# Splitting PSUM copies by bank, spreading routing pieces, and turning token blocks by DMA crossbar in a fused attention and expert kernel

## The chip, the cores and the metric

The kernel runs on one core of a Trainium2 chip. A core has TensorE (PE: matmuls, and transposes as a matmul against an identity), VectorE (DVE), ScalarE (ACT), GpSimd (POOL) and SyncE (SP, which issues DMAs here), each with its own queue of instructions in order, and 16 DMA engines that all of them share. Matmul results land in PSUM, which has eight banks of 512 fp32 columns; everything else lies in SBUF or in HBM. The metric is the device time of one launch in microseconds (us).

## The reference, cut to what matters

Two stages follow each other. The first is attention with random features: for 8 batches and 8 heads of 576 rows by 64, q and k are projected by `omega` (128 features), cosine and sine are taken, and the products with `v` are divided by a row sum. The second routes each of the 4608 rows (512 wide) to one of 8 experts by a cosine score, and applies that expert's two matrices and a gate.

```python
def phi(x):
    proj = np.einsum('bhsd,md->bhsm', x, omega)
    return np.concatenate([np.cos(proj), np.sin(proj)], axis=-1) / np.sqrt(m)
q_p, k_p = (phi(q), phi(k))
kv = np.einsum('bhsm,bhsd->bhmd', k_p, v)
z = np.sum(k_p, axis=2)
num = np.einsum('bhsm,bhmd->bhsd', q_p, kv)
den = np.einsum('bhsm,bhm->bhs', q_p, z)
...   # den is kept away from zero
# x: num / den, laid out as 4608 rows of 8 heads x 64
...
xn = x / (np.linalg.norm(x, axis=-1, keepdims=True) + 1e-06)
logits = xn @ en.T / tau
expert_idx = np.argmax(logits, axis=1)
...   # gate_w: the softmax of the chosen expert
for e in range(E):
    mask = expert_idx == e
    h = np.maximum(x[mask] @ w1[e], 0.0)
    out[mask] = gate_w[mask, None] * (h @ w2[e])
```

## The kernel before: what the change touches

**Attention** runs in 32 steps; a step handles a pair of heads of one batch. The loop is staggered: in step n the matmuls of step n stand beside the finish of n - 1 and the projections of n + 1. For each step, raw rows of q and k are transposed on PE into `qreg`, a PSUM region of nine blocks of 128 columns that begins at a bank's edge, so that columns 0 to 511 are one bank and 512 to 1151 reach over two more. Then they are copied to SBUF, k (with the first q block beside the ninth k block) by one engine and the rest of q by ACT:

```python
def turns(m):
    t = raw.pop(m)
    for j in range(NCH if m + 1 >= 0 else 4):          # NCH = 9
        nc.tensor.transpose(qreg[:, j*P : j*P + P], t[:, j*P : j*P + P], ident)
    ...
def copy_k(m):
    t = pa.tile([P, 5 * P], FP32, tag="kT", name="kT", bufs=1)
    if m + 1 >= 0:
        if m in ROUTED:                                # steps 18 to 30
            nc.scalar.activation(t, qreg[:, 0 : 5 * P], AF.Copy)
        else:
            nc.vector.tensor_copy(t, qreg[:, 0 : 5 * P])
    ...
def copy_q(m):
    t = pa.tile([P, 4 * P], FP32, tag="qT", name="qT", bufs=1)
    nc.scalar.activation(t, qreg[:, 5 * P :], AF.Copy)
```

`proj_k` and `proj_q` multiply these by `omega`; `whole_turns` (ACT) rounds the angle, `frac` (DVE) takes the rest, `fold` (DVE) its magnitude, `wave` (ACT) the sine, for both the sine and the cosine. The finished rows go to an HBM table `x_rows`, 512 fp16 values and a gate each.

**Routing** is small DVE work: `choose` and `choose2` pick the expert, `rank` and `places` give each token a slot, `block_hot` and `row_hot` build one-hot matrices with which PE inverts the placement, `block_experts` gives each block's expert, `root` (POOL) takes norms, `gates_a` to `gates_d` (DVE, with one tanh on ACT) compute the gates, `store_gates` (DMAs on SP) writes them into `x_rows`. It is done twice: for the first four batches, which fill blocks 0 to 10 (K1 = 11), within the attention steps 18 to 31 (`m` = n - 18 in `route_first`); and for all rows in the first expert blocks (`route_second`).

**Experts** follow as 40 blocks of 128 tokens of one expert each (and up to three more in a conditional part, not reached here). Rows are gathered from `x_rows` three to four blocks ahead, transposed on PE, and copied by ACT:

```python
def turn_x(j, eng):
    t = xin.pop(j)
    tr = bank(2 if j < 3 else 2 + 4 * (j % 2)).bitcast(FP16)
    for c in range(4):
        nc.tensor.transpose(tr[:, c*P : c*P + P], t[:, c*P : c*P + P].bitcast(FP16), ident16)
    move(eng, gpos[:, j : j + 1], t[:, D:XW].bitcast(FP32))     # the gate
    xT = late("kq", j % 2, 512)
    move(eng, xT, tr[:, 0:512])
    mo[j] = {"xT": xT}
...
def block(j, end):
    if j + 1 < end:
        hidden(j + 1, "act")        # 32 matmuls, relu by ACT into hT
    route_second_pe(j)
    if j < end - 2:
        turn_x(j + 2, "act")
    route_second(j)
    if j + 4 < NBLK:
        gather(j + 4)               # indirect DMA issued by POOL, three row buffers
    if j in (3, 4):
        for a in range(GRP1 * SG + SG * (j - 3), GRP1 * SG + SG * (j - 2), 3):
            root(a, a + 3)          # POOL
    result(j)                       # 8 matmuls, scaled by the gate on ACT
    if not LAST - 2 <= j < LAST:
        scatter(j)                  # indirect DMA issued by POOL
```

## Time and profile before

| | |
|---|---|
| time, median of 3 runs | 511.17 us (506.64 to 512.13) |
| the profiled execution | 485.76 us, span 483.9 us |
| PE busy | 462.3 us (96%) |
| PE weight loads busy | 387.8 us (80%) |
| POOL busy | 371.5 us (77%) |
| ACT busy | 357.8 us (74%) |
| DVE busy | 298.8 us (62%) |
| HBM traffic | 67.90 MB read, 15.22 MB written |

The span runs from the first to the last instruction of one profiled execution. Busy times of the engines overlap, and each is an average over stages that differ: which engine holds the others up has to be read stage by stage. Matmuls of PE are pipelined, so the duration of one overlaps the next; the time that a group takes is the distance between starts. In an answer that lists instructions, the columns are start, duration, engine, line of the kernel, operation, what it writes and reads, the count, and in square brackets the idle time before it and what ended that. In an answer of waits, a line has the waiting instruction, what it waited for, the total in us, the number of times, and the longest.

### The profile page before, as it was taken

What the parts mean: (1) busy time and instruction counts of PE and PEld (TensorE: products, weight loads), DVE (VectorE), ACT (ScalarE), POOL (GpSimd) and SP (SyncE); (2) the same over time, 40 slices, a digit from 0 to 9 for tenths busy, and PEclk for the clock granted to TensorE, in tenths of its full rate; (3) what the DMA queues carried; (4) which work ended last, traced back from release to release, by engine and by line L of the source; (5) the groups of instructions that cost most, each with busy time, mean ns of one, the idle gap of its engine ahead of it and who ended that gap; (6) DMA issues with size and microseconds to landing.
All of it is one profiled execution on the core that took longest, in us unless ns stands there. A gap on an engine that the chain in (4) does not pass through costs nothing.

```text
span 483.9 us, 18742 instructions
## 1 busy us (share of the span) xinstructions
PE 462.3 (96%) x7924; PEld 387.8 (80%) x7924; DVE 298.8 (62%) x506; ACT 357.8 (74%) x475; POOL 371.5 (77%) x472
## 2 busy tenths in 40 slices
PE   8899999999999999999999999889799999999993
PEld 7788889888888888888888888777577777777771
DVE  3688978889988888998888899969540000000000
ACT  3588788788788779989889979766366666666661
POOL 3599888998899998989999988866956555555552
PEclk9999999999999999999999999999989999999997
DMA  6279888787997878889779778423143223232211
GB/s 178 65 172 195 176 180 167 171 176 156 176 177 164 167 152 200 164 163 180 159 147 185 166 153 148 75 52 112 42 100 132 94 95 104 87 99 103 92 71 35
DMA packets 57652, 65.63 MB, mean 136 GB/s; under 512 B 29397, under 2 KB 37589, under 8 KB 57568
## 3 DMA queue, kind: packets, MB, share of 16 engines
q0 software_dynamic: 18064, 30.96, 33.7%
q1 hardware_dynamic: 39104, 32.95, 26.5%
q8 instruction: 65, 1.06, 0.9%
q10 hardware_dynamic: 400, 0.49, 0.4%
q14 instruction: 19, 0.16, 0.1%
HBM read 67.90 MB, written 15.22 MB: 172 GB/s over the span
## 4 chain that ended last, share of the span: by engine, by line
PE 54%; POOL 18%; DVE 12%; DMA 7%; ACT 5%; issue 3%; POOLq 0%; SPq 0%; ACTq 0%
PE ps L893 13%; PE ps L914 12%; PE ps L388 8%; PE ps L334 6%; POOL zt L321 5%; PE ps L260 4%; PE ps L224 3%; POOL zt L322 3%; POOL zs L324 3%; POOL zs L323 3%; DMA out_dram<-sik,prm 3%; PE ps L272 3%; DVE sik L297 2%; DMA kq<-in_q_dram 2%; DVE siq L297 2%
## 5 line engine op out<-in xcount | busy, mean ns | idle before, releaser
L893 PEld LDWEIGHTS <-w_sb 128*128 x1280 | 75.8, 99 | 10.3 <-issue 1.5
L893 PE MATMUL ps<-kq,w_sb 128*128 128x128 f16 x1280 | 79.0, 220 | 0.7 <-ACT kq L842 0.7
L388 PE MATMUL ps<-kv,siq 128*64 128x73 f32 x1152 | 76.4, 229 | 1.4 <-DVE kv L373 0.6
L914 PE MATMUL ps<-w_sb,cok 128*128 x320 | 76.2, 382 | 0.0
L388 PE MATMUL ps<-kv,coq 128*64 128x73 f32 x1152 | 74.9, 226 | 0.0
L388 PEld LDWEIGHTS ps<-kv,siq 128*64 128x64 f32 x1152 | 60.5, 135 | 5.3 <-ACT xb L422 0.7
L388 PEld LDWEIGHTS ps<-kv,coq 128*64 128x64 f32 x1152 | 61.1, 137 | 0.0
L811 POOL DMA_INDIRECT xin_all<-rf_x,prm x43 | 45.5, 1057 | 17.0 <-PE ps L850 9.6
L321 POOL TENSOR_TENSOR zt<-sik 128x512 f32<-128x512 f32 x32 | 41.2, 1287 | 22.3 <-ACT sik L310 21.9
L914 PEld LDWEIGHTS <-cok 128*128 128x128 f16 x320 | 29.8, 98 | 28.8 <-issue 0.4
L322 POOL TENSOR_TENSOR zt<-zt 128x256 f32<-128x256 f32 x64 | 48.9, 765 | 5.0
L297 DVE SCALAR_TENSOR_TENSOR sik<-sik,ps 128x1152 f32<-128x1152 f32 x32 | 43.2, 1349 | 7.1 <-ACT sik L293 6.9
L260 PE MATMUL ps<-omT,kT 64*128 64x128 f32 x576 | 45.1, 288 | 0.0
L297 DVE SCALAR_TENSOR_TENSOR siq<-siq,ps 128x1152 f32<-128x1152 f32 x32 | 43.1, 1347 | 1.8 <-ACT siq L293 1.7
L321 POOL TENSOR_TENSOR zt<-cok 128x512 f32<-128x512 f32 x32 | 42.8, 1339 | 0.0
L293 ACT ACTIVATE sik<-ps 128x1152 f32<-128x1152 f32 x32 | 36.2, 1132 | 8.1 <-PE ps L260 6.6
L310 ACT ACTIVATE siq<-siq 128x1152 f32<-128x1152 f32 x32 | 37.1, 1160 | 4.3 <-DVE coq L303 4.3
L293 ACT ACTIVATE siq<-ps 128x1152 f32<-128x1152 f32 x32 | 35.9, 1123 | 5.8 <-PE ps L280 5.8
L247 ACT ACTIVATE qT<-ps 128x512 f32<-128x512 f32 x32 | 19.1, 595 | 28.3 <-DVE kT L238 27.9
L260 PEld LDWEIGHTS ps<-omT,kT 64*128 64x128 f32 x576 | 39.1, 192 | 1.1 <-issue 0.5
L310 ACT ACTIVATE coq<-coq,consts 128x1152 f32<-128x1152 f32 x32 | 39.9, 1247 | 0.0
L310 ACT ACTIVATE cok<-cok,consts 128x1152 f32<-128x1152 f32 x32 | 39.9, 1247 | 0.0
(194 smaller groups left out, 1152.3 us busy)
## 6 DMA issues: line engine op xcount, KB each, us to landing
w_sb<-in_moe_w_dram POOLq DMA_DIRECT2D x32, 512.0 KB, 8.2
kq<-in_q_dram SPq DMA_DIRECT2D x62, 144.0 KB, 4.4
kq<-in_k_dram SPq DMA_DIRECT2D x62, 144.0 KB, 4.4
v<-in_v_dram SPq DMA_DIRECT2D x34, 144.0 KB, 3.9
rf_x<-xb SPq DMA_DIRECT2D x32, 144.0 KB, 7.3
xin_all<-in_v_dram SPq DMA_DIRECT2D x30, 144.0 KB, 4.8
xin_all<-rf_x,prm POOLq DMA_INDIRECT x43, 2.9
out_dram<-sik,prm POOLq DMA_INDIRECT x20, 3.0
```

What stands on the lines that cost most here:

```text
L247: nc.scalar.activation(t, qreg[:, 5 * P :], AF.Copy)
L260: nc.tensor.matmul(kreg[:, s * P : s * P + P], lhsT=t[r0 : r0 + 64, j * P : j * P + P], rhs=omT[r0 : r0 + 64], start=True, stop=True,)
L293: nc.scalar.activation(si, REG[nm], AF.Copy, bias=CMAGIC, scale=1.0)
L297: nc.vector.scalar_tensor_tensor(out=si, in0=si, scalar=CMAGIC, in1=REG[nm], op0=ALU.subtract, op1=ALU.subtract)
L310: nc.scalar.activation(t, t, AF.Sin, bias=pio2 if which == "co" else 0.0, scale=-TWO_PI * SINSC)
L321: nc.gpsimd.tensor_tensor(zt, t[:, 0:4], t[:, 4:8], ALU.add)
L322: nc.gpsimd.tensor_tensor(zt[:, 0:2], zt[:, 0:2], zt[:, 2:4], ALU.add)
L334: nc.tensor.matmul(kreg[64 * half : 64 * half + 64, 512 * hh : 512 * hh + P], lhsT=d["v"][r0 : r0 + 64, c], rhs=ph[r0 : r0 + 64, s * P : s ...
L388: nc.tensor.matmul(nm2[r0 : r0 + 64, a, (c - c0) * W : (c - c0) * W + W], lhsT=ph[:, s * P + r0 : s * P + r0 + 64], rhs=d["kv"][:, half, h ...
L811: ins = nc.gpsimd.indirect_dma_start(out=t, out_offset=None, in_=x_rows[:], in_offset=bass.IndirectOffsetOnAxis(ap=prm[:, j : j + 1], axis=0),
L893: nc.tensor.matmul(h_ps[:, f * P : f * P + P], lhsT=weights(k), rhs=d["xT"][:, c * P : c * P + P], start=(c == 0), stop=(c == 3),)
L914: nc.tensor.matmul(y_ps, lhsT=d["hT"][:, c * P : c * P + P], rhs=weights(NW1 + NW2 * (j % 2) + c), start=(c == 0), stop=(c == NW2 - 1),)
```

## The change

It has four parts. The first lets the two copies read different banks side by side, the second and third spread small routing work over steps and blocks, the fourth takes the transposes of the token rows from PE and their copies from ACT.

1. *Copies.* The k copy takes columns 0 to 511 of `qreg` (one bank), the q copy columns 512 to 1151 (two others); the ninth k block and the first q block now travel with q. In the prologue the same split holds, ACT takes part in the first copy, and DVE's copy comes ahead of its `frac`, while `fold` moves into step 0.
2. *First routing.* `block_experts` moves one step earlier, `gates_c` is halved over two steps, `choose` of group 2 moves one step later.
3. *Second routing.* The sums of squares of the last group move from block 2 to block 1, the roots on POOL from blocks 3 and 4 to blocks 0 and 2, and each `row_hot` is cut into three pieces.
4. *Transposes.* Rows of blocks 3 to 39 are transposed by a DMA through the crossbar, SBUF to SBUF, issued by SP in block j for block j + 3, straight into one of four buffers. For these blocks `turn_x` copies only the gate. PE transposes and their PSUM copies stay for blocks 0 to 2.

```diff
@@ -230,36 +230,34 @@
                 )
 
         def copy_k(m):
-            t = pa.tile([P, 5 * P], FP32, tag="kT", name="kT", bufs=1)
+            t = pa.tile([P, 4 * P], FP32, tag="kT", name="kT", bufs=1)
+            if m in ROUTED:
+                nc.scalar.activation(t, qreg[:, 0 : 4 * P], AF.Copy)
+            else:
+                nc.vector.tensor_copy(t, qreg[:, 0 : 4 * P])
+            st.setdefault(m + 2, {})["kT"] = t
+
+        def copy_q(m):
+            t = pa.tile([P, 5 * P], FP32, tag="qT", name="qT", bufs=1)
             if m + 1 >= 0:
-                if m in ROUTED:
-                    nc.scalar.activation(t, qreg[:, 0 : 5 * P], AF.Copy)
-                else:
-                    nc.vector.tensor_copy(t, qreg[:, 0 : 5 * P])
-                st.setdefault(m + 1, {})["t"] = t
+                nc.scalar.activation(t, qreg[:, 4 * P :], AF.Copy)
+                st[m + 1]["qT"] = t
             else:
-                nc.vector.tensor_copy(t[:, 0 : 4 * P], qreg[:, 0 : 4 * P])
-                nc.vector.tensor_copy(t[0:64, 4 * P :], qreg[0:64, 4 * P : 5 * P])
-            st.setdefault(m + 2, {})["kT"] = t
-
-        def copy_q(m):
-            t = pa.tile([P, 4 * P], FP32, tag="qT", name="qT", bufs=1)
-            nc.scalar.activation(t, qreg[:, 5 * P :], AF.Copy)
-            st[m + 1]["qT"] = t
-
+                nc.scalar.activation(t[0:64, 0:P], qreg[0:64, 4 * P : 5 * P], AF.Copy)
+            st[m + 2]["kT8"] = t
 
         KS = [c // 2 + 4 * (c % 2) if c < 8 else 8 for c in range(NCH)]
         QS = [8 if c == 0 else (c - 1) // 2 + 4 * ((c - 1) % 2) for c in range(NCH)]
 
         def proj_k(n):
-            t = st[n]["kT"]
             for j in range(5):
+                t = st[n]["kT"][:, j * P : j * P + P] if j < 4 else st[n]["kT8"][:, 0:P]
                 for par in range(2 if j < 4 else 1):
                     r0 = 64 * par
                     s = j + 4 * par if j < 4 else 8
                     nc.tensor.matmul(
                         kreg[:, s * P : s * P + P],
-                        lhsT=t[r0 : r0 + 64, j * P : j * P + P],
+                        lhsT=t[r0 : r0 + 64],
                         rhs=omT[r0 : r0 + 64],
                         start=True,
                         stop=True,
@@ -272,7 +270,7 @@
                 nc.tensor.matmul(
                     qreg[:, 512 * par : 512 * par + 512],
                     lhsT=omT[r0 : r0 + 64],
-                    rhs=d["qT"][r0 : r0 + 64],
+                    rhs=d["qT"][r0 : r0 + 64, P:],
                     start=True,
                     stop=True,
                 )
@@ -280,7 +278,7 @@
             nc.tensor.matmul(
                 qreg[:, 1024:1152],
                 lhsT=omT[64:P],
-                rhs=d["t"][64:P, 4 * P :],
+                rhs=d["qT"][64:P, 0:P],
                 start=True,
                 stop=True,
             )
@@ -528,6 +526,7 @@
         nc.vector.tensor_scalar(omT, tp_om, INV2PI, None, ALU.mult)
         turns(-2)
         copy_k(-2)
+        copy_q(-2)
         keep_warm(2)
         proj_k(0)
         nc.vector.tensor_scalar(emb_n[:E, 0:1], emb_n[:E, 0:1], 1e-6, None, ALU.add)
@@ -539,10 +538,9 @@
             )
         whole_turns(0, "k")
         turns(-1)
+        copy_k(-1)
         copy_q(-1)
         frac(0, "k")
-        fold(0, "k")
-        copy_k(-1)
         tp_e = ps[:, 6 * 512 : 6 * 512 + H * E]
         for h in range(H):
             nc.tensor.transpose(
@@ -843,15 +841,25 @@
             else:
                 nc.vector.tensor_copy(dst, src)
 
+        def turn_x_dma(j):
+            xT = late("kq", j % 4, 512)
+            nc.sync.dma_start_transpose(
+                out=xT.rearrange("p (c t) -> p c t", c=4), in_=xin[j][:, 0:D].bitcast(FP16)
+            )
+            mo[j] = {"xT": xT}
+
         def turn_x(j, eng):
             t = xin.pop(j)
+            if j in mo:
+                move(eng, gpos[:, j : j + 1], t[:, D:XW].bitcast(FP32))
+                return
             tr = bank(2 if j < 3 else 2 + 4 * (j % 2)).bitcast(FP16)
             for c in range(4):
                 nc.tensor.transpose(
                     tr[:, c * P : c * P + P], t[:, c * P : c * P + P].bitcast(FP16), ident16
                 )
             move(eng, gpos[:, j : j + 1], t[:, D:XW].bitcast(FP32))
-            xT = late("kq", j % 2, 512)
+            xT = late("kq", j % 4, 512)
             move(eng, xT, tr[:, 0:512])
             mo[j] = {"xT": xT}
 
@@ -1010,17 +1018,18 @@
                 gates_b(0, GRP1)
             elif m == 9:
                 row_hot(oh1, r1["lo"], 6, 12)
+                block_experts(0, K1, False, r1["a"])
             elif m == 10:
                 row_hot(oh1, r1["lo"], 12, S1)
-                block_experts(0, K1, False, r1["a"])
+                gates_c(0, 1)
             elif m == 11:
                 rows_of(r1["inv"], 0, K1, r1["a"])
-                gates_c(0, GRP1)
+                gates_c(1, GRP1)
             elif m == 12:
                 gates_d(0, GRP1)
                 store_gates(0, GRP1)
+            elif m == 13:
                 choose(GRP1)
-            elif m == 13:
                 square_rows(GRP1)
                 choose2(GRP1)
 
@@ -1050,10 +1059,12 @@
                 nc.tensor.addr_align(128, STEP_AT)
             if n < NS:
                 proj_q(n, place_first if n == NS - 1 else lambda: None)
+                fold(n, "k")
+                if n == 0:
+                    wave(n, "si", "k")
+                whole_turns(n, "q")
                 if n > 0:
-                    fold(n, "k")
-                whole_turns(n, "q")
-                wave(n, "si", "k")
+                    wave(n, "si", "k")
                 zsum(n, 0)
             if n == 0:
                 set_up_turn()
@@ -1160,6 +1171,7 @@
             elif j == 1:
                 squares(NS - 1, nc.vector)
                 square_sums(NS - 1)
+                square_rows(NGRP - 1)
                 r2["rk"] = r2["a"].take((NSLOT + 1) * E).rearrange("p (e s) -> p e s", e=E)
                 nc.vector.tensor_copy(r2["rk"], r2["ps"])
                 starts2(r2["rk"], NSLOT, r2["a"])
@@ -1167,13 +1179,14 @@
             elif j == 2:
                 r2["dest"] = places2(*r2["wg"], NSLOT, r2["a"])
                 r2["blk"], r2["lo"] = places3(r2["dest"], NSLOT, r2["a"])
-                square_rows(NGRP - 1)
             elif j == 3:
                 r2["rr"] = block_hot(r2["blk"], NSLOT, K1, NBLK - K1, r2["a"])
             elif j == 4:
-                row_hot(r2["oh"][0], r2["lo"][:, 0:18], 0, 18)
+                for a in range(0, 18, 6):
+                    row_hot(r2["oh"][0], r2["lo"][:, 0:18], a, a + 6)
             elif j == 5:
-                row_hot(r2["oh"][1], r2["lo"][:, 18:36], 0, 18)
+                for a in range(0, 18, 6):
+                    row_hot(r2["oh"][1], r2["lo"][:, 18:36], a, a + 6)
                 for part in (gates_a, gates_b, gates_c, gates_d):
                     part(GRP1, NGRP)
                 store_gates(GRP1, NGRP)
@@ -1188,10 +1201,12 @@
             if j < end - 2:
                 turn_x(j + 2, "act")
             route_second(j)
+            if 2 < j + 3 < LAST:
+                turn_x_dma(j + 3)
             if j + 4 < NBLK:
                 gather(j + 4)
-            if j in (3, 4):
-                for a in range(GRP1 * SG + SG * (j - 3), GRP1 * SG + SG * (j - 2), 3):
+            if j in (0, 2):
+                for a in range((GRP1 + j // 2) * SG, (GRP1 + j // 2 + 1) * SG, 3):
                     root(a, a + 3)
             result(j)
             if not LAST - 2 <= j < LAST:
```

More of the change, by code (lines that the diff above doesn't have):

```diff
@@ L232, in copy_k @@
         def copy_k(m):
-            t = pa.tile([P, 5 * P], FP32, tag="kT", name="kT", bufs=1)
-            if m + 1 >= 0:
-                if m in ROUTED:
-                    nc.scalar.activation(t, qreg[:, 0 : 5 * P], AF.Copy)
-                else:
-                    nc.vector.tensor_copy(t, qreg[:, 0 : 5 * P])
-                st.setdefault(m + 1, {})["t"] = t
-            else:
-                nc.vector.tensor_copy(t[:, 0 : 4 * P], qreg[:, 0 : 4 * P])
-                nc.vector.tensor_copy(t[0:64, 4 * P :], qreg[0:64, 4 * P : 5 * P])
+            t = pa.tile([P, 4 * P], FP32, tag="kT", name="kT", bufs=1)
+            if m in ROUTED:
+                nc.scalar.activation(t, qreg[:, 0 : 4 * P], AF.Copy)
+            else:
+                nc.vector.tensor_copy(t, qreg[:, 0 : 4 * P])
             st.setdefault(m + 2, {})["kT"] = t
         def copy_q(m):
-            t = pa.tile([P, 4 * P], FP32, tag="qT", name="qT", bufs=1)
-            nc.scalar.activation(t, qreg[:, 5 * P :], AF.Copy)
-            st[m + 1]["qT"] = t
+            t = pa.tile([P, 5 * P], FP32, tag="qT", name="qT", bufs=1)
+            if m + 1 >= 0:
+                nc.scalar.activation(t, qreg[:, 4 * P :], AF.Copy)
[3 more added lines that the diff above has]
+            st[m + 2]["kT8"] = t
         KS = [c // 2 + 4 * (c % 2) if c < 8 else 8 for c in range(NCH)]
```

## The prediction

> **What bounds the kernel now.** I read the page first: the slices of the span show one engine full nearly throughout.
>
> ```profile
> PE   8899999999999999999999999889799999999993
> ...
> DVE  3688978889988888998888899969540000000000
> ...
> DMA  6279888787997878889779778423143223232211
> ```
>
> TensorE (PE) is at nine tenths except at the start, at slices 25, 26 and 28, counted from 0 (within 302 to 351 us) and at the end. Slices 0 to 25 are the attention, the rest the expert blocks; in the latter the DMA engines are a third busy. The answer by windows gives the same for the steady expert blocks; its columns are busy time and count per engine, the clock, the DMA share and GB/s.
>
> ```profile
> 360.00:400.00 40.00, 40.00 (x468) 29.61 (x466) 0.00 (x0) 26.43 (x54) 23.50 (x23) 1.00 0.31 102
> 400.00:440.00 40.00, 40.00 (x471) 29.77 (x469) 0.00 (x0) 26.42 (x55) 22.44 (x22) 1.00 0.30 99
> ```
>
> PE is busy all 40 us of 40, ScalarE (ACT) 26, GpSimd (POOL) 23. What a block consists of is read from the timeline, starts in the first column:
>
> ```profile
> 440.25 1.95 PE L893 MATMUL ps<-kq,w_sb 128*128 128x128 f16 x32
> ...
> 441.42 1.01 POOL L941 DMA_INDIRECT out_dram<-siq,prm  x1 [1.39 <-ACT siq L934]
> ...
> 442.04 0.39 PE L850 MATMUL ps<-ident,xin_all 128*128 128x128 f16 x4
> ...
> 442.26 1.89 PE L914 MATMUL ps<-w_sb,cok 128*128 x8
> ...
> 442.73 1.03 POOL L811 DMA_INDIRECT xin_all<-rf_x,prm  x1 [0.30 <-PE ps L850]
> ...
> 443.99 1.95 PE L893 MATMUL ps<-kq,w_sb 128*128 128x128 f16 x32
> ```
>
> From start to start: first product 442.04 - 440.25 = 1.79 us, the four transposes 442.26 - 442.04 = 0.22 us, second product 443.99 - 442.26 = 1.73 us. A block is 3.74 us, and all of it is PE issuing back to back. So here each PE instruction removed is time removed.
>
> The ramp of the expert stage is different. From the waits and the timelines of 316 to 362 us:
>
> ```profile
> DVE lsq L150 <- POOL lsq L762: 4.7, 1, 4.7
> ```
> ```profile
> 335.95 1.87 POOL L811 DMA_INDIRECT xin_all<-rf_x,prm  x1 [0.30 <-PE ps L850]
> 337.85 4.92 POOL L762 TENSOR_TENSOR lsq<-lsq,pmh 128x3 f32<-128x3 f32 x3
> 342.95 2.52 POOL L941 DMA_INDIRECT out_dram<-siq,prm  x1 [0.18 <-issue]
> 345.77 1.03 POOL L811 DMA_INDIRECT xin_all<-rf_x,prm  x1 [0.30 <-PE ps L893]
> ```
> ```profile
> 350.60 0.40 PE L850 MATMUL ps<-ident,xin_all 128*128 128x128 f16 x4 [2.94 <-DMA xin_all<-rf_x,prm]
> 350.93 2.62 PE L914 MATMUL ps<-w_sb,cok 128*128 x8
> 353.34 2.92 PE L893 MATMUL ps<-kq,w_sb 128*128 128x128 f16 x32
> ```
>
> The square roots (L762) sit on POOL between two gathers, so block 8's gather starts only at 345.77; PE waits 2.94 us for it and then runs some matmuls at a lower clock. First product 7 starts at 344.66; with 1.79 + 36 inversions (1.1) + 0.22 + 1.73 the next would start at 349.5, but it starts at 353.34 and lasts about 1 us too long: **4.8 us lost**. The same roots hold VectorE (DVE) 4.7 us, and with it the gates; their store is issued from 352.83 by SyncE (SP).
>
> In attention the starts of the q projection (L272) follow each other by 9.22 us in most steps, with PE full. Summing what exceeds 9.22 over the steps gives 6.5 us: 0.5 in step 1, 2.3 in step 28, where DVE's routing delays PE, the rest in crumbs.
>
> **What the Trainium skill says.** "Advanced Engine Details and Errata", section "X-Bar Transpose (TRN2)": transposing DMAs run about as fast as plain ones, 350 to 400 GB/s; no transposing DMA is in this trace. "VectorE: DVE Perf Modes", section "The three transpose paths": 390 ns on TensorE against 1309 ns by crossbar for one 128x128; here a PE transpose shows 219 ns and costs 54 ns of issue. "SBUF — State Buffer", section "SBUF: two separate sides": while VectorE holds the shared port, GpSimd can't write DMA descriptors; the trace agrees: a gather or scatter takes 1.03 us alone, but 1.87 and 2.52 us beside DVE's long compares at 335 to 345 us. "TensorE: Matmul & The Clock Gate", section "Why this matters for your kernels": an idle gap over some 3 us lowers the clock; here 2.92 us instead of 1.95 after the gap.
>
> **The change, part by part.**
>
> 1. Transposes. 37 blocks (3 to 39) lose four PE transposes and one PSUM copy on ACT (0.6 us, off the path). On PE 37 x 0.215 = 8.0 us. Blocks 10 to 37 of the loop are steady: 28 x 0.215 = 6.0 us, which I count in full, at 3.52 us a block. The other nine (1.9 us) lie in the ramp, where a wait decides.
>
> Does the added DMA stay hidden? The gather of rows j+4 is issued about 2.3 us into block j (439.00 against 436.68) and lands 2.9 us later by the page: 1.7 us into block j+1. There SP issues the transpose; the first product needs it at the start of block j+3. At 3.52 us a block this leaves 2 x 3.52 - 1.7 = 5.3 us. A transpose moves 128 KB; at 350 GB/s that is 0.4 us, plus a fixed part which I take from the gathers' 2.9 us: 3 to 3.5 us, an estimate. It fits, and the DMA engines have two thirds free.
>
> 2. Ramp. The roots move to blocks 0 and 2, and row_hot is cut from 2304 to 768 columns an instruction, so POOL gets in between. That removes DVE's wait of 4.7 us: DVE ends its compares at about 344.8, and the gates (0.8 before the tanh, 0.4 on ACT, 2.1 after) end at about 348.3 instead of 352.8. But SP works in order, and in block 5 the four gate stores stand ahead of the transpose of block 8. They are issued from 348.4 and take 2.6 us (352.83 row: 2.58), so that transpose leaves at 351 and lands at 354. First product 8 then starts at about 354 where it started at 353.3. **A wait takes the place of the one removed**: with the 1.9 us of the nine PE transposes included, I book the ramp as 0.5 us worse.
>
> 3. Copies. The split at column 512 makes k read one PSUM bank and q two others. Before:
>
> ```profile
> ACT qT L247 <- DVE kT L238: 27.9, 18, 2.1
> ```
>
> ACT gets that back, and 0.1 us of longer copy per step against it. But those are steps at PE's 9.22 us, so nearly nothing of the 27.9 us is on the path. I book 0.7 us. At the start the q projection no longer waits for DVE's fold and copy: it can follow the warming matmuls at 13.2 instead of 13.84, and ACT does the first sine while it waits; 1.0 us.
>
> 4. First routing. Moving block_experts (2.0 us on DVE with its long last write) from step 28 to 27 takes it away from the inversion on PE, but lays it on step 27, where DVE has 0.4 + 1.1 us free. 0.8 us won. Choose goes into step 31 with choose2: 0.3 us lost.
>
> Sum: 6.0 - 0.5 + 0.7 + 1.0 + 0.8 - 0.3 = 7.7 us of the span. The timed median is 511.17 against 485.76 in the profiled run, 5% more. If the extra is slower PE, the gain grows with it to 8.1 us. Since the parts look tuned together, my ramp is more likely too dark than too bright; I add 1 us: 511.2 - 9 = **502 us**.
>
> **Rivals.**
>
> A. The crossbar doesn't keep up. If a transpose of 128x512 costs four times the skill's 1.3 us and they queue, the block becomes 5.2 us, and 30 blocks add 30 x 1.5 = 45 us: 550 us. The skill's bandwidth and the 30% DMA share speak against it; nothing in this trace can exclude it. A milder form: latency of 6 us, past the 5.3 us of slack; PE then waits some tenths every block and the 6 us are gone: 509.
>
> B. The ramp is better than I think: if the gates end earlier or the store's issue is shorter, most of the 4.8 us and the 1.9 us comes home: 496 to 497.
>
> C. POOL becomes the bound of the ramp: roots in block 2 coincide with DVE's 1.36 us multiplies and push the gathers of blocks 7 and 8 back by 3 us, to which the transpose's 3 us add: 506. The 4.92 us for three roots speak for it.
>
> **Range and chances.** Main case 500 to 504 (half), B 496 to 499 (a fifth), C and the milder A 505 to 510 (a fifth), A in full (a tenth or less). Medians differ by a few us among runs of the same kernel (506.64 to 512.13). Eight in ten: 495 to 510. Two per cent is 10.2 us, so below 501: 0.42 faster, 0.50 the same, 0.08 slower.
>
> **What would show it.** In the changed profile: PE transposes (L850 before) 12 instead of 160; blocks 3.52 us apart with PE full in the windows after 370 us; a transpose from issue to landing of 3 to 3.5 us; in block 7 a PE wait for the transpose of block 8, issued after the gate stores; no DVE wait for the roots; ACT's wait of 27.9 us gone with the attention steps still at 9.22 us. Wrong would be: blocks at 3.7 us or more with PE waiting for SP's DMA; gathers slowed by the transposes; no wait in block 7; attention steps shorter than 9.2 us.

## The result, and the profile after

| | us, median | range |
|---|---|---|
| kernel before | 511.65 | 506.64 to 512.39 |
| changed kernel | 488.12 | 486.59 to 489.71 |

The ratio is 0.956, interval 0.949 to 0.963: 23.5 us won, where I had forecast 9. The time lies below my range of 495 to 510.

Each later set of runs was made on one chip with the kernel before beside it, and that kernel took 487 us in some sets (483.6 to 495.3) and 508 us in others (504 to 516), without overlap; I call them **quick sets** and **slow sets**, and the comparison above is like a slow set.

The page of the changed kernel, slices of the span (PE, DVE, DMA as before):

```profile
PE   8999999999999999999999999788889999989992
...
DVE  3789788799878788989888998859620000000000
...
DMA  6299798897887888887878777325566464545541
```

PE is no fuller than in the page of before, DMA went from a third to a half in the expert blocks. The transposes are there as intended: 12 PE transposes instead of 160, and 37 by the crossbar. The span, 487.0 us, is even longer than the 483.9 of the page of before. So **the two pages don't show the gain at all**: the page of before is that of an execution that took 485.76 us, while the timed ones took 511. A window of the changed kernel (busy time and count for PE, PEld, DVE, ACT and POOL, clock, DMA share, GB/s):

```profile
400.00:440.00 40.00, 37.90 (x426) 27.31 (x425) 0.00 (x0) 19.36 (x44) 22.26 (x22) 1.00 0.53 130
```

PE has gaps of 2.1 us in 40, where before it had none. What was missing was a profile of the kernel before in a slow set. Experiment e9 below gave one, with a span of 511.1 us. The same window of it:

```profile
400.00:440.00 40.00, 36.31 (x410) 25.86 (x408) 0.00 (x0) 22.21 (x47) 19.28 (x20) 1.00 0.26 85
```

PE idles 3.7 us of 40, at a full clock. The starts of the first expert product of block 0, of block 10 and of block 39 cut each span in four:

| profile | to block 0 | blocks 0 to 10 | blocks 10 to 39 | one block | after 39 |
|---|---|---|---|---|---|
| before, its first page (like a quick set) | 314.4 | 47.4 | 108.4 | 3.74 | 13.7 |
| before, slow set (e9) | 320.5 | 50.0 | 126.9 | 4.38 | 13.7 |
| changed, its first page (the runs above) | 313.7 | 51.0 | 107.2 | 3.69 | 15.2 |
| changed, slow set (e5) | 311.5 | 52.8 | 106.4 | 3.67 | 15.1 |
| changed, quick set (e13) | 315.1 | 47.8 | 102.7 | 3.54 | 13.7 |

Of 24.1 us between the second row and the third, 19.8 come from the 29 steady blocks. The rest is 6.8 in attention (4.3 of it in two steps of 12.41 and 10.88 us, which take 9.39 and 9.60 in the first page of before; e12, of the same set as e9, doesn't have them), less 1.0 in the ramp and 1.5 at the end.

**Where the steady blocks lose 0.6 us.** The first page of before, one block; lines as in the prediction:

```profile
427.09 0.39 PE L850 MATMUL ps<-ident,xin_all 128*128 128x128 f16 x4
...
427.35 0.60 ACT L903 ACTIVATE cok<-ps 128x512 f16<-128x512 f32 x1 [0.30 <-PE ps L893]
...
427.94 0.59 ACT L842 ACTIVATE kq<-ps 128x512 f16<-128x512 f16 x1
...
429.04 1.67 PE L893 MATMUL ps<-kq,w_sb 128*128 128x128 f16 x27
```

L903 is the relu of the second half of a first product. ACT works in order, so the copy of turned rows (L842) stands behind it. The copy ends at 427.94 + 0.59 = 428.53, and PE needs it at 429.04: a slack of **0.5 us**, which I had not looked for because PE waited for nothing. The same stretch in the slow set (e9):

```profile
425.94 0.39 PE L850 MATMUL ps<-ident,xin_all 128*128 128x128 f16 x4
...
427.09 0.60 ACT L903 ACTIVATE cok<-ps 128x512 f16<-128x512 f32 x1 [1.19 <-PE ps L850]
...
427.83 0.60 ACT L842 ACTIVATE kq<-ps 128x512 f16<-128x512 f16 x1
...
428.48 1.95 PE L893 MATMUL ps<-kq,w_sb 128*128 128x128 f16 x32 [0.42 <-ACT kq L842]
```

The relu starts 1.15 us after the first transpose instead of 0.26, so 0.9 us later, the copy ends at 428.43, and PE starts 0.05 us after it, having waited. Nothing is slower in itself: the relu 0.60, the copy 0.60, the product 1.95 as before. Over the whole run, the waits of e9:

```profile
ACT cok L903 <- PE ps L850: 32.9, 28, 1.7
...
PE ps L893 <- ACT kq L842: 18.5, 34, 1.6
```

The steady blocks differ by 126.9 - 108.4 = 18.5 us. That PE's waits for the copy sum to 18.5 us as well is chance: 12.7 us of them (28 waits) lie in the steady blocks, the rest before, and a wait is counted only from the modelled end of the last matmul ahead of it. In the first page of before the same PE wait is 0.7 us, once.

**The relu is not the whole of it, and not the last to hold the copy.** The copy also waits for PE's signal that the transposes are done, and the traces keep the times of these signals. I give medians over the steady blocks, measured from the end of the work that the profile gives:

| | first product done | transposes done | second product done | transposes' end to next first product |
|---|---|---|---|---|
| before, first page | 0.01 | 0.01 | 0.01 | 1.56 = 0.01 + 0.45 + copy 0.59 + 0.51 |
| before, slow set (e9) | 0.90 | 1.41 | 0.01 | 2.14 = 1.41 + 0.08 + copy 0.60 + 0.05 |

In the first page the copy waits 0.45 us behind the relu, and 0.51 us are left over at the end. In e9 the signal of the transposes is late too, and in 27 of 29 blocks the copy starts 0.08 us after it; the relu has ended 0.05 us ahead of that signal. So the relu and the signal hold the copy for almost the same time, and the signal comes last. The 0.58 us between 1.56 and 2.14 are what a block becomes longer (median 4.30 against 3.74). The ends of matmuls are modelled in a profile, so it can't be told whether the work was done late or only its signal came late; but the second product, which follows both in PE's order, signals on time.

And the changed kernel in its first page. L911 is now the second relu, and the copy is gone:

```profile
442.35 2.06 PE L901 MATMUL ps<-kq,w_sb 128*128 128x128 f16 x32
443.44 0.60 ACT L911 ACTIVATE cok<-ps 128x512 f16<-128x512 f32 x1 [2.43 <-PE ps L922]
...
444.25 1.89 PE L922 MATMUL ps<-w_sb,cok 128*128 x8
```

This relu belongs to the product that began at 438.84 and gave way to the second product at 440.62; it starts 2.8 us after that, so it is even later. But PE doesn't wait for it at 442.35: that product reads the rows from the crossbar's buffer. The relu's output is read only by the second product at 444.25. The change did not make the signals punctual; it took the rows off the way from PE over a late signal and a copy on ACT back to PE.

### The profile page after: what moved, and what is told of

Its sections match the earlier page's. It is cut to its first block, busy times and chain, and to the rows that moved or that the text cites. A ratio compares the mean times of both kernels' runs of the same rounds, so it can differ in the third digit from the quotient of the medians.

```text
span 487.0 us, 18456 instructions
## 1 busy us (share of the span) xinstructions
PE 458.4 (94%) x7776; PEld 380.9 (78%) x7776; DVE 294.9 (61%) x511; ACT 341.6 (70%) x439; POOL 369.6 (76%) x472
## 3 DMA queue, kind: packets, MB, share of 16 engines
q8 instruction: 64, 1.05, 0.9%
## 4 chain that ended last, share of the span: by engine, by line
PE 67%; POOL 16%; DVE 5%; DMA 4%; issue 3%; ACT 2%; SPq 0%; POOLq 0%; ACTq 0%; DVEq 0%
PE ps L901 14%; PE ps L922 13%; PE ps L386 10%; PE ps L332 9%; PE ps L258 6%; PE ps L224 5%; POOL zt L319 5%; PE ps L270 4%; POOL zt L320 3%; POOL zs L321 3%; DMA kq<-xin_all 3%; POOL zs L322 2%; PE ps L361 2%; PE ps L353 2%; POOL xb L422 1%
## 5 line engine op out<-in xcount | busy, mean ns | idle before, releaser
L901 PEld LDWEIGHTS <-w_sb 128*128 x1280 | 75.0, 98 | 19.9 <-issue 11.4
L901 PE MATMUL ps<-kq,w_sb 128*128 128x128 f16 x1280 | 79.9, 219 | 8.2 <-DMA kq<-xin_all 3.7
L386 PE MATMUL ps<-kv,siq 128*64 128x73 f32 x1152 | 77.8, 231 | 1.4 <-DVE kv L371 0.6
L386 PE MATMUL ps<-kv,coq 128*64 128x73 f32 x1152 | 76.2, 228 | 0.0
L386 PEld LDWEIGHTS ps<-kv,siq 128*64 128x64 f32 x1152 | 61.4, 137 | 5.2 <-ACT siq L291 0.7
L911 ACT ACTIVATE cok<-ps 128x512 f16<-128x512 f32 x40 | 24.0, 600 | 38.9 <-PE ps L901 21.3
L949 POOL DMA_INDIRECT out_dram<-siq,prm x20 | 20.6, 1028 | 39.0 <-ACT siq L942 37.8
L291 ACT ACTIVATE siq<-ps 128x1152 f32<-128x1152 f32 x32 | 36.2, 1131 | 15.1 <-PE ps L278 15.1
L319 POOL TENSOR_TENSOR zt<-cok 128x512 f32<-128x512 f32 x32 | 43.5, 1359 | 0.0
L909 ACT ACTIVATE cok<-ps 128x512 f16<-128x512 f32 x40 | 23.9, 596 | 21.3 <-PE ps L901 19.7
```

Of the source, the lines that this page charges most:

```text
L291: nc.scalar.activation(si, REG[nm], AF.Copy, bias=CMAGIC, scale=1.0)
L319: nc.gpsimd.tensor_tensor(zt, t[:, 0:4], t[:, 4:8], ALU.add)
L386: nc.tensor.matmul(nm2[r0 : r0 + 64, a, (c - c0) * W : (c - c0) * W + W], lhsT=ph[:, s * P + r0 : s * P + r0 + 64], rhs=d["kv"][:, half, h ...
L901: nc.tensor.matmul(h_ps[:, f * P : f * P + P], lhsT=weights(k), rhs=d["xT"][:, c * P : c * P + P], start=(c == 0), stop=(c == 3),)
```

## Experiments

**Theory** (called the theory of the queue in some expectations): the gain is ACT's copy leaving the queue behind the late relu. **Rivals**: the transposes' own signal being late, so that the copy is held wherever it stands; the 8 us of PE work; the spread of the small work (parts 1 to 3); PE's fetching of instructions or the loads of expert numbers as the cause of the lateness; a crossbar that costs or gives something of its own.

### Four parts in a quick set: e1 to e4

e1 is the kernel before once more. e2 is the changed kernel without part 4:

```diff
-            if 2 < j + 3 < LAST:
-                turn_x_dma(j + 3)
```

e3 is the kernel before with part 4 alone (`turn_x_dma`, the early return in `turn_x`, four buffers, the two lines above), e4 the kernel before with part 1 alone.

> The kernel before, unchanged. Its profile took 485.8 us, its timed executions 506 to 512, while the changed kernel takes 487 to 490 with and without a profile. Theory 1 (the lost time of the timed executions lies in the program before itself, in a stage that the first profile happened to run without loss): a new profile shows about 505 to 512 us, and the windows show where, most likely in the expert blocks, longer than 3.74 us with PE waiting for nothing shown. Theory 2 (the first profile is an accident of another kind, such as another chip): profile and times both near 486 or both near 511 here, with every stage stretched by the same share.

> The changed kernel with PE transposes and PSUM copies for all blocks: parts 1 to 3 alone. If the crossbar transposes bring the gain (theory A): 506 to 509 us, near the kernel before. If the copies and the routing pieces bring it (theory B): 488 us or less, since in the profiles the expert blocks of the changed kernel are not shorter than before (3.7 us on average from 357 to 474 us, with PE waits of 0.3 to 0.75 us in them that nothing shown ends). If the size of PE's program matters (theory C, instruction fetch): times that follow neither, with PE waits for nothing shown in the profile.

> The kernel before with part 4 alone: crossbar transposes for blocks 3 to 39. Theory A: about 490 us. Theory B: 511 us or more, since the ramp with late roots and the transposes behind the gate stores is longer by some us. Theory C: PE waits in the expert blocks like those of the changed kernel, 0.3 to 0.75 us in every second block.

> The kernel before with part 1 alone: copies split at the bank's edge and the new order of the prologue. My prediction gave it 1.7 us. Theory A: 509 to 510 us. Theory B: 495 us or less, if the wait of 27.9 us of ACT for DVE's copy was what stretched the timed executions.

| | us | before | ratio and interval | blocks 0 to 10 | one block |
|---|---|---|---|---|---|
| e1 | 487.44 | 486.96 | 0.9996 (0.9972 to 1.0020) | 45.6 | 3.80 |
| e2 parts 1 to 3 | 481.95 | 486.96 | 0.9886 (0.9820 to 0.9952) | 44.8 | 3.74 |
| e3 part 4 | 487.40 | 486.96 | 1.0016 (0.9987 to 1.0046) | 54.8 | 3.52 |
| e4 part 1 | 486.51 | 486.96 | 0.9973 (0.9944 to 1.0002) | 45.7 | 3.80 |

Here the kernel before takes 487 us, not 511, and no part brings more than 6 us. That was the first sign that the gain isn't in the parts but in what they meet. Part 4 makes the blocks exactly as short as forecast, 3.52 us, and loses it all in the ramp. The waits of e3 show why (L903 is the first product there):

```profile
PE ps L903 <- DMA kq<-xin_all: 12.8, 2, 10.6
```

With the roots still late, SP issues the gate stores at 353.42, the transpose of block 8 leaves behind them at 356.13, and PE waits 10.6 us for it.

### The same in a slow set: e5 to e8

e5 is the changed kernel once more. e6 has parts 1 to 3, PE transposes as before, and the 37 crossbar transposes beside them into a buffer that nobody reads. e7 moves the crossbar transpose ahead of the routing piece, so ahead of the gate stores in SP's queue. e8 is the changed kernel with PE's instructions shifted against its fetches from block 7 on.

```diff
 # e6: crossbar transposes go to slots 2 and 3, PE's copies to 0 and 1
-            xT = late("kq", j % 4, 512)          # in turn_x_dma
-            mo[j] = {"xT": xT}
+            xT = late("kq", 2 + j % 2, 512)
-            xT = late("kq", j % 4, 512)          # in turn_x
+            xT = late("kq", j % 2, 512)
 # e7
-            route_second(j)
             if 2 < j + 3 < LAST:
                 turn_x_dma(j + 3)
+            route_second(j)
 # e8, first lines of block(j)
+            if j == 7:
+                nc.tensor.addr_align(256, 160)
```

> The changed kernel, unchanged, beside the kernel before on the chip of this call. So far parts 1 to 3 alone gave 482 us, part 4 alone 487, the kernel before 487. Theory D (the 4.4% belong to how the kernel before ran where it took 511, not to the program): the two kernels stand at 484 to 489 us here, ratio 0.99 to 1.01. Theory A (the change as a whole is worth 4%): a ratio near 0.956.

> Parts 1 to 3 with PE transposes, and beside them the 37 crossbar transposes into a buffer that nobody reads. It measures what the transfers cost others. If they cost nothing (my prediction): 482 us, as without them. If they delay PE's own instructions or the gathers (theory E): 485 to 490 us, with PE waits for nothing shown, or for gathers, in the expert blocks, which were clean at 3.74 us a block without them.

> The changed kernel with the crossbar transpose issued ahead of the routing piece of its block, so that block 8's no longer stands behind the four gate stores in block 5. If the gate stores hold it (my step 2 of the ramp): PE's wait for the transpose in block 7 goes, 2 to 5 us faster than the changed kernel. If the wait in block 7 comes from elsewhere (rows gathered late, the inversion waiting for DVE): no difference of more than 1 us.

> The changed kernel with PE's program padded once, at the start of block 7, so that what PE meets [...] (about every two blocks in the profile of the changed kernel, always within the first product) falls into the second product, where PE issues an instruction per 216 ns and has time. Theory C (PE waits for its own instructions): the waits for nothing shown from 370 us on vanish and the time falls by up to 5 us. If the waits come from something else: they stay where they are.

| | us | before | ratio and interval | blocks 0 to 10 | one block |
|---|---|---|---|---|---|
| e5 changed | 488.54 | 508.0 | 0.9568 (0.9506 to 0.9629) | 52.8 | 3.67 |
| e6 unread crossbar | 510.29 | 508.0 | 1.0016 (0.9988 to 1.0044) | 49.3 | 4.58 |
| e7 transpose ahead of gates | 483.79 | 508.0 | 0.9541 (0.9484 to 0.9598) | 46.4 | 3.67 |
| e8 shifted | 495.93 | 508.0 | 0.9709 (0.9647 to 0.9770) | 61.4 | 3.67 |

e5 repeats the gain. e6 has everything of the change except that the rows are still turned on PE and copied by ACT, and nothing is left of the gain: PE waits 25.8 us for that copy. Both of its expectations, 482 and 485 to 490 us, missed: they were made from the quick set. So the gain hangs on who brings the rows, not on parts 1 to 3. Its blocks (4.58) are longer than those of the kernel before (4.38), so the unread transposes may cost something; parts 1 to 3 quite alone weren't run in a slow set, and could be some us better than e6.

e7 has the lowest median of this set. Its profile shows the wait that the prediction named for the gate stores. From e5, then from e7:

```profile
347.39 3.49 SPq L798 DMA_DIRECT2D rf_x<-gate  x4
...
354.52 3.57 PE L901 MATMUL ps<-kq,w_sb 128*128 128x128 f16 x32 [6.16 <-DMA kq<-xin_all]
```
```profile
343.19 1.21 SPq L846 DMA_TRANSPOSE kq<-xin_all  x1
...
353.75 3.47 PE L901 MATMUL ps<-kq,w_sb 128*128 128x128 f16 x32 [2.24 <-DMA kq<-xin_all]
```

In e7 the transpose of block 8 leaves before the stores, and block 8 starts at 347.83 instead of 354.52 without a wait. A smaller wait for the next block's transpose, 2.24 us, remains. The ramp is 6.4 us shorter in the profiles. The medians of e5 and e7 differ by 4.7 us, but their ratios only by 0.0027, or 1.4 us, with intervals that overlap: how much time this order is worth isn't settled.

e8 was to test whether PE's fetches make the signals late. Its blocks stay as they are, and one PE wait of 11.5 us before block 8, for nothing that the profile shows, makes it slower. It says nothing for that rival and doesn't exclude it, as one shift isn't all shifts.

### Is it the copy, or the crossbar? e9 to e12

e9 is the kernel before, for its profile. e10 has parts 1 to 3 and no crossbar transposes, with the gate and the turned rows copied by DVE from block 10 on; e11 is the kernel before with that one edit; e12 is the kernel before with the loads of the expert numbers left out from block 10 on, so that all later blocks use the expert of block 9 and the output is not the reference's.

```diff
 # e10 (in the changed kernel without turn_x_dma's call) and e11 (in the kernel before)
-                turn_x(j + 2, "act")
+                turn_x(j + 2, "act" if j < 8 else "dve")
 # e12
-                expert_of(j + 2)
+                if j < 8:
+                    expert_of(j + 2)
+                else:
+                    eoff[j + 2] = eoff[j + 1]
```

> The kernel before once more, for its profile. So far one chip ran it in 487 us (A) and another in 508 us (B), and the changed kernel in 488.5 us on B. In the profile of the crossbar-unused run on B the blocks take 4.5 us; PE's signal for the end of the first product comes about 1.1 us later than its matmuls, the second relu starts late, ACT's copy of the turned rows behind it too, and PE waits for that copy (25.8 us in 34 waits). Theory F (late signals meet a chain without slack in the kernel before): where it takes about 508 us, its blocks are near 4.4 us with the same wait; where it takes about 487 us, 3.74 us and no such wait.

> Parts 1 to 3 with PE transposes, but from block 10 on the turned rows and gates are copied by DVE, which is idle there, instead of ACT, so that this copy no longer stands behind the second relu. Theory F: 480 to 484 us on A and on B alike, so about 5% below the kernel before on B, without any crossbar transpose. Theory A (the crossbar itself brings the gain on B): 505 us or more on B, 482 on A.

> The kernel before with that one edit alone: copies of turned rows by DVE from block 10 on. Theory F: 485 to 489 us on either chip, 0.95 to 0.96 of the kernel before on B, which would put the whole measured gain on this chain. Theory A: no change on either chip.

> The kernel before, leaving out PE's loads of each block's expert number from block 10 on (those blocks use the expert of block 9, so the output is not the reference's). If these loads into PE's registers make PE's signals late on B: about 487 us there. If not: 505 us or more on B. On A: 487 us under either.

| | us | before | ratio and interval | blocks 0 to 10 | one block |
|---|---|---|---|---|---|
| e9 before, one run | 512.98 | 508.32 | | 50.0 | 4.38 |
| e10 pieces, DVE copies | 489.45 | 508.32 | 0.9595 (0.9515 to 0.9675) | 46.5 | 3.79 |
| e11 DVE copies alone | 497.99 | 508.32 | 0.9697 (0.9593 to 0.9801) | 48.8 | 3.88 |
| e12 no expert loads | 507.73 | 508.32 | 0.9976 (0.9910 to 1.0043) | 48.4 | 4.42 |

e10 has no crossbar and all PE transposes, and comes to 0.9595, about as far as the change itself (0.9568, in another set), though at 489.45 us it misses the 480 to 484 expected. A window, one block and the waits of e10:

```profile
400.00:440.00 40.00, 40.00 (x456) 28.89 (x454) 5.34 (x22) 19.41 (x31) 21.75 (x22) 1.00 0.30 99
```
```profile
399.79 0.39 PE L858 MATMUL ps<-ident,xin_all 128*128 128x128 f16 x4
...
401.32 0.42 DVE L842 COPY kq<-ps 128x512 f16<-128x512 f16 x1 [3.31 <-PE ps L858]
...
401.80 1.95 PE L901 MATMUL ps<-kq,w_sb 128*128 128x128 f16 x32
```
```profile
ACT cok L911 <- PE ps L858: 17.2, 20, 0.9
...
PE ps L901 <- ACT kq L840: 2.4, 2, 1.7
```

PE is full again, and its wait for ACT's copies is down to 2.4 us, from blocks that ACT still copies. The relu is still often late (17.2 us in 20 times), and it no longer matters. But DVE's copy is not free of lateness either. DVE has idled for 3.31 us with nothing ahead of the copy, and still starts it only 1.14 us after the transposes' end at 399.79 + 0.39 = 400.18: **DVE takes the transposes' signal late as well**, by 1.12 us (median; 1.11 in e11). So the theory of the queue doesn't explain the gain of e10. It comes in time because the signal is 0.29 us less late than in e9, the copy follows it after 0.02 us instead of 0.08, and DVE copies in 0.42 us instead of 0.60: 1.12 + 0.02 + 0.42 + 0.05 = 1.61 us from the transposes' end to the product, where it was 2.14 in e9 and 1.56 fit without a wait. Why the signal is less late there isn't shown.

e11 confirms the direction with one edit, but at 498 it stays above the 485 to 489 that were expected: its profiled execution, of 505.32 us, has blocks of 3.88 us but reaches block 0 only at 328.4. Of the 14.1 us that this is later than in the first page of before, 9.8 lie in two attention steps of 14.76 and 14.07 us (9.39 and 9.60 there), before the edit takes effect; its other runs took 490.7 to 500.0. e12 keeps blocks of 4.42 us and PE's wait for the copy (18.8 us): the loads of expert numbers are not what makes the signals late.

### The whole change in a quick set, and two more ways around the queue: e13 to e18

e13 is the changed kernel, e14 parts 1 to 3 alone, as e2. e15 and e17 are the kernel before with the second relu on DVE from block 9 on; e16 and e18 leave it on ACT, but put both relus behind the copy.

```diff
 # e15, e17
-                hidden(j + 1, "act")
+                hidden(j + 1, "act" if j < 8 else "dve")
 # e16, e18: the relus of hidden() as a function of their own, from block 9 on called after turn_x
+            if j >= 8 and j + 1 < end:
+                relus(j + 1, "act")
```

> The changed kernel once more, for the comparison with the kernel before on the chip of this call. If the kernel before takes 505 to 512 us here (its steady blocks at about 4.4 us): 488, a ratio of 0.957. If it takes 487 (blocks at 3.74 to 3.80): by the separate parts there, 0.989 for parts 1 to 3 and nothing for the transposes, 482 to 484. A rival, that the crossbar transposes cost something of their own next to parts 1 to 3, expects 487 or more in the second case.

> The changed kernel without part 4: parts 1 to 3 alone, transposes on PE. Where the kernel before takes 505 to 512: it keeps the copy of turned rows behind the late relu on ACT, so blocks stay at 4.4 us and only the ramp and the attention gain: 500 to 509 by the theory of the queue. A rival, that the spread routing pieces are what brings the time, expects 488 to 492. Where the kernel before takes 487: 482 for both.

> The kernel before, the relu of the second half of each first product on DVE instead of ACT from block 9 on. By the theory of the queue the copy of turned rows then stands behind nothing that is late, and waits for the transposes alone: blocks of 3.75 to 3.9 us and 485 to 492 where the kernel before takes 505 to 512; DVE's relu itself starts late by the same 0.9 us if TensorE's signal is late for every engine. If only ACT takes the signal late, DVE's relu starts within 0.1 us of the product's end. The rival, that the transposes' own signal is as late, expects ACT's copy to start 1 us late all the same: blocks of 4.2 us or more, 502 to 510.

> The kernel before, both relus left on ACT but from block 9 on put behind the gate and the copy of turned rows in ACT's queue. By the theory of the queue the copy no longer waits for the end of the first product but for the transposes, which end 0.2 us later on PE; so it starts hardly earlier than now unless the signals of the transposes come in time: 485 to 495 if they do, and 504 to 512 with blocks of 4.3 us or more if the signal of any group of matmuls comes about a microsecond late. Where the kernel before takes 487, 484 to 492, as the relus come 0.8 us later but are needed only a block later.

> The kernel before with the second relu on DVE from block 9 on, once more. Where the kernel before takes 505 to 512 us (blocks of 4.4 us): by the theory of the queue 485 to 495, blocks of 3.75 to 3.9 us; by the rival, that the transposes' own signal comes about 1 us late too, 502 to 510 with blocks of 4.2 us or more. DVE's relu late by 0.9 us: TensorE's signal is late for every engine; within 0.1 us: only ACT takes it late. Where the kernel before takes 487 us, it again shows nothing: 486 to 490.

> The kernel before with both relus behind the copy of turned rows on ACT from block 9 on, once more. Where the kernel before takes 505 to 512 us: 485 to 495 if the transposes' signal comes in time, 502 to 512 if it is late as well. Where it takes 487 us, 486 to 490.

| | us | before | ratio and interval |
|---|---|---|---|
| e13 changed | 484.73 | 487.25 | 0.9918 (0.9883 to 0.9952) |
| e14 parts 1 to 3 | 482.42 | 487.25 | 0.9879 (0.9797 to 0.9961) |
| e15 second relu on DVE | 488.92 | 487.25 | 1.0028 (0.9995 to 1.0062) |
| e16 copy ahead of relus | 488.00 | 487.25 | 0.9985 (0.9942 to 1.0028) |
| e17 as e15 | 485.85 | 486.56 | 0.9993 (0.9972 to 1.0015) |
| e18 as e16 | 486.80 | 486.56 | 0.9993 (0.9964 to 1.0021) |

All of them fell into quick sets. e13 therefore fills the empty cell: **where PE's signals are punctual, the whole change brings 0.8%**, 0.0082 x 487 = 4.0 us, against 4.3% in a slow set. e15 to e18 could only show that their orders cost nothing when nothing is late. They were to tell whether the order within ACT alone would repair a slow set, and whether DVE takes PE's signals late. The second is answered by e10: it does. For the first, e9 speaks against it, as its copy starts right at the late signal of the transposes; no run in a slow set tests it.

The ramp of e14 shows what the spread roots are worth when no crossbar follows (L901 is the first product of blocks 7 and 8):

```profile
345.58 1.95 PE L901 MATMUL ps<-kq,w_sb 128*128 128x128 f16 x32
...
350.37 1.95 PE L901 MATMUL ps<-kq,w_sb 128*128 128x128 f16 x32
```

From product 7 to product 8 it is 4.79 us, where the prediction's lines of before have 353.34 - 344.66 = 8.68.

## Why the prediction was wrong, point by point

**The step that failed** is the last one before the sum was turned into a time: "The timed median is 511.17 against 485.76 in the profiled run, 5% more. If the extra is slower PE, the gain grows with it to 8.1 us." The extra 25 us were no slower PE. As far as e9 stands for those runs, PE's clock is full in its window and its products last 1.95 us as before. Most of the extra is the steady blocks, 18.5 us longer because PE waits for the rows' copy, which the profiled execution doesn't have; part 4 removes that wait as a side effect. What I had counted is worth about 4 us (e13); the rest of the 23.5 us is luck, from a wait that I had not seen. Behind it stands the reading "A block is 3.74 us, and all of it is PE issuing back to back", which is true of the profile and not of the timed runs. I booked the copies on ACT as "0.6 us, off the path"; they had 0.5 us of slack, and in a slow set they are on the path.

The other steps can be held against a quick set, which is what I had worked them out from: e13 against the first page of before, 4.6 us of span where I had 7.7.

- **Steady transposes, 6.0 us**: right. Blocks 10 to 39 fell from 108.4 to 102.7 us, so 5.7, and in e3 to 102.0.
- **Crossbar hidden, 3 to 3.5 us from issue to landing**: right within 0.1 us for the median, though block 8's, on which the ramp hangs, took 3.5 us (e5) to 5.4 us (the changed kernel's first page). (The gather issued at 439.00 goes out 2.5 us into its block, not 2.3, as that block began at 436.52 and not at 436.68; 5.2 us were left where I had 5.3.) The list of DMA issues of e13 has a median of 3.6 us, and after 370 us PE waits for it once, 0.6 us:

```profile
kq<-xin_all SPq DMA_TRANSPOSE x37, 3.6
```

  Two steady blocks of e13 then start 430.43 - 426.92 = 3.51 us apart:

```profile
426.92 1.95 PE L901 MATMUL ps<-kq,w_sb 128*128 128x128 f16 x32
...
430.43 1.95 PE L901 MATMUL ps<-kq,w_sb 128*128 128x128 f16 x32
```

  Rival A therefore falls. In slow sets the blocks are 3.67 to 3.69 on average.

- **Ramp, 0.5 us worse**: right in size in the quick set, 47.4 to 47.8; against the 50.0 of e9 it was 1.0 us longer in the changed kernel's first page and 2.8 in e5. The mechanism is shown by e14 (43.5 us without the crossbar, so the spread roots win 3.9) and by e7. The wait lands where it can: on block 8 with 6.16 us in e5, on blocks 7 and 8 with 2.23 and 1.05 us in e13. In the changed kernel's first page:

```profile
349.49 2.61 SPq L798 DMA_DIRECT2D rf_x<-gate  x4
...
352.21 10.38 SPq L846 DMA_TRANSPOSE kq<-xin_all  x4
...
357.64 1.95 PE L901 MATMUL ps<-kq,w_sb 128*128 128x128 f16 x32 [1.70 <-DMA kq<-xin_all]
```

  I had put these at 348.4, 351 and 354. The first two are within 1.2 us. The third is 3.6 late: 1.2 us from the issue, and 2.4 us because the transpose landed 5.4 us after it instead of 3; PE waits 1.70 us for it. Without that wait the product would have started at 355.94, as the second product ahead of it took 3.36 us instead of 1.89 and began late, with PE idling by 0.3 to 0.5 us at a time among the inversions.

- **Copies, prologue, first routing, 2.2 us**: right where I looked, lost after it. The q projection of step 0 starts at 13.18 (I had 13.2) instead of 13.84; steps 0 and 1 win 0.5 us each; ACT's 27.9 us wait for DVE's k copy is gone and the step's floor is still 9.23 us. Instead there is, in the changed kernel's first page:

```profile
ACT qT L243 <- PE ps L224: 12.2, 18, 1.2
```

  The last q projection starts 2.0 us earlier there and 3.0 in e13. But the first expert product comes 0.7 us earlier and 0.8 later, respectively. The gain is spent between the two, where choose and the sums of squares of group 2 now stand; that it is they is argued from the order of the code, not shown.
- **One us added because "my ramp is more likely too dark"**: not borne out, and small.
- **Rival B** (a ramp that comes home) is what e7 and e14 do, with 46.4 and 43.5 us; the change as it is doesn't. **Rival C** fell: the roots are no longer in the way.

What stays open is why PE's signals come late in slow sets: 0.9 us for the first product and 1.4 for the transposes before the change, up to 3 us for the first product after it. It isn't the expert loads (e12) nor the crossbar's load on the DMAs (e9 has none). The five later sets, on five chips, were each quick or slow as a whole, so it seems to go with the chip or something that lasts on it, not with the kernel; no chip was measured twice.

## What to carry to other kernels

Before a profile is read, hold its execution time against the timed median; when they differ by 5%, as here, the profile may show another bottleneck than the one that is timed, and a second profile is worth more than a closer look at the first. In a loop in which one engine is full, list the slack of each chain that leaves it and comes back through another engine: the smallest one (0.5 us here) is what a late signal turns into the bound. Then ask what the late link waits for last. An engine's order and a late signal can hold it for almost the same time (0.05 us apart in e9), and only the copy on an engine with nothing ahead of it (e10) told them apart. When transfers are moved to an engine's DMA queue, look at what already stands in that queue: one line's order (e7) took 6.4 us off the ramp of the profile, though only 1.4 to 4.7 us of it show in the times, and not clear of noise.

## What the runs showed of the hardware that I had not expected

- The same kernel takes 487 us in some sets and 508 us in others, a ratio of 1.04, with full clock and equal durations of instructions in the steady blocks; what differs there is how late PE's signals come: 0.01 us against 0.90 us after the first product, and 0.01 against 1.41 us after the transposes (medians over blocks, first page of before and e9). ACT and DVE both take them late (e9, e10).
- A crossbar transpose of 128 KB takes 3.6 us from issue to landing and 1.19 us of SP's queue, but much DMA time: with the share of the 16 engines at 0.58 in e13's windows and 3.51 us a block, 0.58 x 16 x 3.51 = 32.6 engine-us a block; before it was 0.305 x 16 x 3.74 = 18.3. The difference of 14.3 for 131 KB is 9.2 GB/s an engine, 147 GB/s for 16. It is an estimate and on the low side, as the packets of gathers and scatters beside them became longer too. The Trainium skill, "Advanced Engine Details and Errata", section "X-Bar Transpose (TRN2)", on which the prediction leaned, has 350 to 400 GB/s; by this estimate it is less than half in this pattern.
- PE waits now and then for nothing that the profile shows, in attention steps that otherwise repeat to 0.01 us: 9.36 us became 13.91 in one step of e1, 9.39 became 12.41 in one of e9 (the first times are those of the first page of before). In both the DMA queue for instructions has a packet that comes 6 to 7 us later than in the first page of before (124.42 against 117.53 us, 198.40 against 192.39), and PE goes on 1.4 us after its end. That points to the fetching of instructions; no run tests it, and the wait of 11.5 us in e8 doesn't follow this pattern.
